# Other numbers in a list scheduler's priority table: a gated recurrence and a low-rank mixer on one core

## The chip, the cores and the metric

The kernel runs on one core of one Trainium2 chip. The metric is the device time of one execution in microseconds (us). Five runs of the kernel before gave 699.36 us in the median, from 696.82 to 702.98. PE is TensorE's matmul stream, PEld its weight loads, DVE is VectorE, ACT is ScalarE, POOL is GpSimd, and SP is the engine that issues most DMAs.

## The reference

```
# attention: q, k, v, a_re, a_im are (4, 8, 768, 48) = batch, heads, seq, dim
mag = sqrt(a_re^2 + a_im^2);  scale = min(mag, 0.999) / (mag + 1e-6)
a = (a_re + i a_im) * scale
for t in range(768):
    S = a[t][:, None] * S + k[t] v[t]^T          # a complex 48x48 state per head
    y[t] = q[t] . Re(S)
# mixer: x = y as (4, 768, 384); U (768, 32), V (32, 768), w_ch1 (384, 1536), w_ch2 (1536, 384)
u = x + ((x^T @ U) @ V)^T
out = u + relu(u @ w_ch1) @ w_ch2
```

All is in 32 bit floats.

## The kernel before

**How the work is cut.** Each of the 4 batches has 768 steps in 6 chunks of 128, so there are 24 chunks, numbered through. Two chunks form a group of gates, so there are 12 groups, and also one unit `m` of the mixer (256 tokens), so there are 12 of those.

For a group, `gates` turns a_re and a_im into the logarithm of the magnitude (tile `GL`) and the angle. Sums of the logarithms are matmuls with fixed triangles (`es ps`, L606, and `tot`, L635), of which ACT takes the exponential (tiles `es` and `E`). Sums of the angles are matmuls too (`ph`, L673 and L676), and ACT takes sine and cosine (tile `cs`). The exponential and the sine need different tables, so ACT loads a table (L345) twice for each group. Four small DMAs of SP (L621) bring `E` into the tile `T`.

For a chunk, `prep` multiplies q and k by `es` and by `cs` on DVE (tiles `qk` and `QKC`), turns them by PE transposes (`tr`, L728), and ACT copies them to `QK` (L731). There is one QKC buffer, so the product for k has to wait for the transposes of q. Then `chain` does the chunk itself:

- a first inner product (`inner`, L762), DVE steps that multiply parts of QK by T (L351), a second inner product, more such steps, a third, more, the corner blocks (`corners`, L812), and one more
- transposes of k (`ks ps`, L834), copied by ACT (L836), and the change of the state (`dk`, L849), which DVE adds up in `GM` and `G`
- the output (`y`, L880 from inside the chunk, L888 from the state), copied by ACT to the tile `xo` (L897)

From group 5 on, the two chunks of a group go through their inner products together.

When all six chunks of a batch are there, the mixer of its three units can begin: `mixed` (L922 and L938) for the low-rank part, a transpose (`uTp`, L951), the first product (`up`, L963, or a form with fewer products, `few`, L1021, in the last six units), the relu on ACT, the second product (`down`, L1109 for the first unit and L1152 for all others), and the sum on DVE.

The two mixer weights come from HBM in 13 pieces, each loaded to `stage` by SP (L501), put through six DVE steps (L510 to L520) and a DMA of POOL (L523).

**What sets the order.** Nothing is emitted as it is written down. Every step is put on a list by `plan.add`, with an engine, a cost, a rank, and what it reads and writes. `Plan.order` then plays the list through: at each moment an engine takes, among the steps that are ready and whose buffers are free, the one with the smallest rank, and prefers, within a margin, one of PE's steps that doesn't change the way the array is split. A step's rank is `urgency(kind, n)`:

```
def urgency(kind, n):
    if kind == "load":
        return n - 20
    if kind in ("totals", "place"):
        return n - 100
    if kind in ("small", "mixing"):
        return n + (1000 if kind == "mixing" else -1000)
    return URGENCY[kind][n]
```

So the products of the mixer come after all else, its small steps before all else, and the rest by the table `URGENCY`, whose kinds are `gates`, `sums` and `angles` (by the first chunk of a group or part), `prep` and `turn`, `levels`, `rest`, `state` and `outs` (by chunk, along the chain), `w1` and `w2` (the steps on the weights), and the loads: `weights` (by piece), `a` (by group), `qk` and `v` (by chunk).

Two things are laid into the order besides. Until the mixer begins, a gap of PE in the plan is filled with a matmul of ones that nothing reads (`spare`, L1276). And the plan holds PE back where a block of 127 of its matmuls would begin before its instruction packet can be there; the five constants for that are `(95, 127, 16, 3.7, 5.0)`.

After that the order of each engine's instructions is fixed.

Of the kernel before, what the change touches and what calls it, by code (L numbers as in the profile page):

```python
# [23 lines left out]
BLK = 32  # L24

URGENCY = {
    "w1": {0: 4.35, 1: 40.16, 2: 150.67, 3: 966.97, 4: 354.88, 5: 201.91, 6: -347.74},
    "w2": {0: 36.04, 2: 316.12, 4: -116.9, 6: 49.42, 8: 239.47, 10: -42.68, 12: 905.56},
    "gates": {0: 106.25, 1: 103.41, 2: -49.5, 4: 87.42, 6: 520.33, 8: -217.02, 10: -47.21, 12: 15.35, 14: 388.43,
        16: 377.04, 18: 75.51, 20: 482.53, 22: -570.43},  # L30
    "angles": {0: -45.95, 1: -31.03, 2: 3.04, 4: 76.17, 6: 325.92, 8: 170.31, 10: -242.52, 12: 333.98, 14: 307.48,
        16: 245.66, 18: -154.27, 20: -22.54, 22: -152.79},
    "prep": {0: 65.38, 1: 12.93, 2: 208.72, 3: -93.77, 4: 100.03, 5: 121.08, 6: 30.53, 7: 497.07, 8: 443.41, 9: 441.88,
        10: 412.66, 11: 327.28, 12: 178.27, 13: 244.54, 14: 74.83, 15: 119.83, 16: 67.35, 17: -210.69, 18: -7.09,
        19: 410.77, 20: -32.17, 21: -59.68, 22: -53.53, 23: 128.41},
    "levels": {0: 41.9, 1: 191.08, 2: 116.73, 3: -50.42, 4: -431.96, 5: -261.25, 6: 94.9, 7: 88.8, 8: -34.01, 9: -85.63,
        10: 13.38, 11: -90.78, 12: -81.71, 13: 119.77, 14: 111.08, 15: 93.04, 16: 48.04, 17: -35.61, 18: -111.26,
        19: 131.26, 20: 11.83, 21: -81.39, 22: -354.36, 23: -91.29},
    "rest": {0: 81.99, 1: -59.7, 2: 1.02, 3: -71.43, 4: 245.98, 5: -217.29, 6: 387.39, 7: 33.15, 8: 464.42, 9: 534.03,
        10: 131.9, 11: -138.5, 12: -136.14, 13: -61.57, 14: -83.99, 15: 843.33, 16: -109.93, 17: 326.93,  # L40
        18: 109.25, 19: -126.18, 20: -0.61, 21: 112.93, 22: -121.98, 23: 76.32},
    "weights": {0: 19.13, 1: -30.23, 2: 81.23, 3: -41.37, 4: 117.09, 5: -154.67, 6: -18.47, 7: -64.05, 8: -71.98, 9: 42.5,
        10: 22.71, 11: -132.3, 12: -28.92},
    "sums": {0: 38.2, 1: 9.35, 2: -20.87, 4: 72.92, 6: -208.53, 8: 13.55, 10: 442.28, 12: 493.43, 14: -34.3,
        16: 584.57, 18: -52.23, 20: -15.92, 22: -382.44},
    "a": {1: 45.05, 2: -60.04, 3: 40.52, 4: -64.28, 5: 71.14, 6: 56.18, 7: 48.88, 8: 43.59, 9: -113.18, 10: -203.48,
        11: 104.55},
    "qk": {0: 21.45, 1: 43.5, 2: -122.7, 3: -37.56, 4: 55.46, 5: 70.35, 6: 197.75, 7: -64.38, 8: 55.95, 9: -154.84,
        10: 75.22, 11: 59.13, 12: 41.58, 13: -8.32, 14: 0.07, 15: -156.61, 16: -54.3, 17: 82.1, 18: -45.58,
        19: -38.55, 20: -58.21, 21: 74.41, 22: 51.81, 23: -3.13},  # L50
    "v": {0: 31.24, 1: -88.34, 2: 92.21, 3: -206.6, 4: -98, 5: 49.22, 6: -34.84, 7: -104.15, 8: 159.93, 9: -122.83,
        10: 61.89, 11: 6.88, 12: 23.97, 13: -44.49, 14: 154.22, 15: 99.08, 16: -48.69, 17: 42.73, 18: -7.23,
        19: 11.85, 20: 11.56, 21: 93.39, 22: 1.68, 23: -27.47},
    "turn": {0: -319.93, 1: 75.52, 2: 97.21, 3: 432.88, 4: 142.09, 5: -31.81, 6: -88.04, 7: -136.12, 8: 41.72,
        9: -25.02, 10: -97.74, 11: -37.55, 12: -241.47, 13: 125.07, 14: -2.5, 15: 87.38, 16: 496.92, 17: -60.29,
        18: 165.32, 19: 552.82, 20: -140.53, 21: 352.69, 22: -223.28, 23: -132.58},
    "state": {0: 945.95, 1: 68.62, 2: 97.42, 3: -70.11, 4: -126.07, 5: -341.17, 6: 128.62, 7: -437.25, 8: 381.46,
        9: 162.75, 10: 823.03, 11: 2.59, 12: -328.28, 13: 333.79, 14: 63.94, 15: 11.18, 16: -228.67, 17: -30.22,
        18: 32.15, 19: -51.58, 20: 49.2, 21: -57.99, 22: -91.91, 23: 89.63},
    "outs": {0: -76.21, 1: 313.36, 2: 356.44, 3: -123.39, 4: 110.21, 5: 113.85, 6: 125.94, 7: -188.23, 8: -30.2,  # L60
        9: -59.92, 10: -1.69, 11: 531.17, 12: -190.52, 13: -532.31, 14: 53.16, 15: -0.59, 16: 32.72, 17: 44.86,
        18: 355.55, 19: 48.52, 20: -58.05, 21: -67.97, 22: 105.42, 23: 31.35},
}


# [1266 lines left out]
```

## Time and profile before

| | us |
|---|---|
| median of 5 runs | 699.36 (696.82 to 702.98) |
| the profiled execution | 701.22 |
| its span, first to last instruction | 699.5 |
| mean granted TensorE clock in it | 0.993 |
| DVE: products on QK (L351), 120 of 1.219 us | 145.5 |
| PE: `up` (L963), 432 records | 98.9 |
| PE: `down` (L1152), the largest form, 396 records | 74.4 |
| PE: `spare` (L1276), 202 records | 53.6 |
| ACT: table loads (L345), 24 of 1.283 us | 30.8 |
| instruction packets (queue q8): 92 packets | 1.51 MB |

A 32-bit matmul of the program shows as two records on PE, a transpose as one. Records are pipelined and their ends are modelled, so a share of busy time on PE isn't a share of its peak. "issue" in a chain of waits is time in which an engine waited for nothing that the profile shows.

### The profile page before, as it was taken

The numbers are of one execution on the slowest core, as the hardware profiler recorded it, in microseconds if no ns is written. First come the engines' busy times: TensorE is split into PE (matmuls) and PEld (weight loads), VectorE is DVE, ScalarE is ACT, GpSimd is POOL, SyncE is SP. The second block draws the span as 40 slices with busy tenths as digits, with TensorE's granted clock in tenths as the row PEclk, the third lists the DMA queues.
The fourth block names the chain that finished last, engine by engine and source line by source line (L and its number), as shares of the span: only waits on it lengthen the run. The fifth ranks groups of instructions, "written<-read, shape, count | busy, mean of one in ns | idle before, by whom it ended". The sixth has DMA issues, their size and how long they took to land.

```text
span 699.5 us, 26207 instructions
## 1 busy us (share of the span) xinstructions
PE 678.6 (97%) x11736; PEld 567.1 (81%) x11736; DVE 541.5 (77%) x886; ACT 415.2 (59%) x776; POOL 47.6 (7%) x84
## 2 busy tenths in 40 slices
PE   9989998999999999999999999999999999999998
PEld 3455666667678888888888888889999999899998
DVE  6899998967997877849769568869887787455734
ACT  7789766667796895857757884642534315131230
POOL 3100000002010010101001010000000000000000
PEclk9999999899999999999999999999999999999999
DMA  7857865657723541431432222131121000000000
GB/s 189 158 162 151 165 131 151 130 136 187 135 63 69 108 100 31 86 65 50 79 74 57 57 53 55 18 76 42 28 43 35 14 29 16 18 7 23 7 18 23
DMA packets 165200, 53.19 MB, mean 76 GB/s; under 512 B 154016, under 2 KB 160352, under 8 KB 165088
## 3 DMA queue, kind: packets, MB, share of 16 engines
q1 hardware_dynamic: 161008, 42.26, 27.6%
q0 software_dynamic: 4080, 9.27, 5.9%
q8 instruction: 92, 1.51, 0.9%
q14 instruction: 20, 0.16, 0.1%
HBM read 33.59 MB, written 4.72 MB: 55 GB/s over the span
## 4 chain that ended last, share of the span: by engine, by line
PE 77%; DVE 11%; ACT 7%; issue 3%; DMA 1%; SPq 1%; DVEq 0%; ACTq 0%
PE down L1152 19%; PE few L1021 12%; PE up L963 11%; PE tr L728 6%; PE inner L762 5%; DVE QK L351 3%; PE y L888 3%; PE dk L849 3%; ACT gate L348 3%; PE spare L1276 2%; PE down L1109 2%; PE ph L673 2%; PE es ps L606 2%; PE ks ps L834 2%; PE y L880 2%
## 5 line engine op out<-in xcount | busy, mean ns | idle before, releaser
L351 DVE TENSOR_TENSOR QK<-QK,T 112x1024 f32<-112x1024 f32 x120 | 145.5, 1219 | 6.8 <-PE corners L812 4.7
L963 PE MATMUL up<-uT,w 128*128 128x256 f32 x432 | 98.9, 381 | 0.2 <-DVE uT L953 0.2
L963 PEld LDWEIGHTS up<-uT,w 128*128 128x128 f32 x432 | 80.3, 190 | 12.1 <-DVE uT L953 0.7
L731 ACT COPY QK<-tr 112x512 f32<-112x512 f32 x96 | 53.2, 587 | 36.2 <-PE tr L728 35.8
L1152 PE MATMUL down<-w,h 128*128 128x192 f32 x396 | 74.4, 331 | 0.0
L348 ACT ACTIVATE gate<-gate 128x768 f32<-128x768 f32 (+1 forms) x91 | 70.3, 791 | 3.6 <-DMA gate<-in_a_re_dram 2.2
L1152 PEld LDWEIGHTS down<-w,h 128*128 128x128 f32 x396 | 63.9, 190 | 2.8 <-issue 1.1
L1029 ACT COPY h<-few 128x512 f32<-128x512 f32 x36 | 20.7, 582 | 74.0 <-PE few L1021 67.3
L762 PEld LDWEIGHTS inner<-QK 112*32 112x32 f32 x4608 | 45.1, 109 | 18.5 <-issue 8.1
L728 PE MATMUL tr<-ident,QKC 128*112 128x128 f32 x384 | 55.0, 280 | 3.3 <-DVE QKC L351 1.9
L354 DVE TENSOR_TENSOR h<-few,h 128x512 f32<-128x512 f32 x54 | 36.9, 690 | 27.3 <-PE few L1021 26.0
L762 PE MATMUL inner<-QK 112*32 112x16 f32 (+1 forms) x4608 | 50.5, 190 | 4.9 <-issue 1.9
L1276 PE MATMUL spare<-ones 128*128 128x512 bf16 x202 | 53.6, 402 | 1.2 <-DVE ones L412 1.2
L728 PEld LDWEIGHTS tr<-ident,QKC 128*112 128x112 f32 x384 | 42.1, 135 | 13.8 <-ACT QK L731 4.7
L351 DVE TENSOR_TENSOR QKC<-qk,cs 128x768 f32<-128x768 f32 x48 | 45.8, 954 | 7.5 <-PE tr L728 7.2
L354 DVE TENSOR_TENSOR xo<-down,xo 128x192 f32<-128x192 f32 (+1 forms) x79 | 29.5, 386 | 21.9 <-PE down L1152 21.6
L897 ACT COPY xo<-y 64x192 f32<-64x192 f32 x96 | 30.0, 312 | 24.6 <-PE y L888 19.3
L1021 PE MATMUL few<-gate,w 128*128 128x128 f32 x336 | 43.0, 277 | 0.0
L768 DVE COPY_PREDICATED DG<-mask,inner 128x128 f32<-128x128 int32 (+1 forms) x72 | 24.1, 342 | 24.1 <-PE inner L762 24.0
L1096 POOL DMA_DIRECT2D out_dram<-xo x32 | 17.9, 560 | 331.6 <-DVE xo L354 315.6
L348 ACT ACTIVATE h<-h 128x512 f32<-128x512 f32 x36 | 22.6, 631 | 30.0 <-DVE h L354 29.9
L1021 PEld LDWEIGHTS few<-gate,w 128*128 128x128 f32 x336 | 39.9, 192 | 0.3
(132 smaller groups left out, 1264.9 us busy)
## 6 DMA issues: line engine op xcount, KB each, us to landing
stage<-in_moe_w_ch_dram SPq DMA_DIRECT2D x12, 768.0 KB, 7.4
gate<-in_a_re_dram SPq DMA_DIRECT2D x24, 192.0 KB, 3.6
gate<-in_a_im_dram SPq DMA_DIRECT2D x24, 192.0 KB, 3.7
qk<-in_q_dram SPq DMA_DIRECT2D x24, 192.0 KB, 3.9
qk<-in_k_dram SPq DMA_DIRECT2D x24, 192.0 KB, 4.2
VP<-in_v_dram SPq DMA_DIRECT2D x24, 192.0 KB, 3.7
T<-E SPq DMA_DIRECT2D x48, 96.0 KB, 2.6
w<-stage POOLq DMA_DIRECT2D x12, 384.0 KB, 5.9
```

The lines of the kernel that those rows point to most:

```text
L348: return nc.scalar.activation(out=o, in_=i, func=f, **kw)
L351: nc.vector.tensor_tensor(out=o, in0=a, in1=b, op=OP.mult)
L354: nc.vector.tensor_tensor(out=o, in0=a, in1=b, op=OP.add)
L728: nc.tensor.transpose(out=get(*ps)[0:DQ, j], in_=get(*qkc)[:, hh * HH + j].rearrange("p u d -> p (u d)")[:, 0:DQ], identity=ident)
L731: ACT(c_act(HH * CH) - 0.05, RT, lambda u=u, hh=hh, ps=ps: nc.scalar.copy(out=get(*QK)[:, u, hh * HH:(hh + 1) * HH], in_=get(*ps)[0:DQ]), ...
L762: nc.tensor.matmul(out=get(*ps)[js, h], lhsT=k_of(h)[:, js], rhs=part(q_of(h)[:, js], "p"), start=True, stop=True, tile_position=(0, j * BLK))
L768: nc.vector.copy_predicated(out=to, mask=part(mask[:, n], "p").unsqueeze(1).to_broadcast(list(to.shape)), data=a if hf < 8 else a.rearrang ...
L897: ACT(c_act(HH * D), RO, lambda r=r, u=u: nc.scalar.copy(out=get(*xi).rearrange("p (a u d) -> p a u d", u=2, d=D)[r * HC:(r + 1) * HC, :, ...
L963: nc.tensor.matmul(out=get(*ps)[:, e], lhsT=w1[:, f, (ff + e) * 128:(ff + e + 1) * 128], rhs=get(*uT)[:, f], start=(f == 0), stop=(f == KD ...
L1021: nc.tensor.matmul(out=get(*ps)[:, q], lhsT=w()[:, q * 128:(q + 1) * 128], rhs=v[0](), start=(n == 0 and q == 0), stop=True, skip_group_ch ...
L1152: nc.tensor.matmul(out=get(*to)[:, part], lhsT=x(j), rhs=y[:, j], start=(first and j == 0), stop=(j == KH - 1), skip_group_check=not first)
L1276: nc.tensor.matmul(out=spare[0], lhsT=ones, rhs=ones.unsqueeze(1).to_broadcast([128, 4, 128]), start=True, stop=True)
```

## The change

Only the table `URGENCY` is changed, and in it every number. No step is added, taken away or costed otherwise; the constants of the plan, the pools and the tiles stay. The kinds and their indices stay too. Some of the lines (the others are changed in the same manner):

```diff
 URGENCY = {
-    "w1": {0: 4.35, 1: 40.16, 2: 150.67, 3: 966.97, 4: 354.88, 5: 201.91, 6: -347.74},
-    "w2": {0: 36.04, 2: 316.12, 4: -116.9, 6: 49.42, 8: 239.47, 10: -42.68, 12: 905.56},
...
+    "w1": {0: -262.78, 1: 77.4, 2: 59.79, 3: 354.47, 4: 165.29, 5: 432.04, 6: 13.21},
+    "w2": {0: -278.56, 2: 142.74, 4: 90.26, 6: -29.83, 8: 309.38, 10: -293.7, 12: 259.97},
...
-    "weights": {0: 19.13, 1: -30.23, 2: 81.23, 3: -41.37, 4: 117.09, 5: -154.67, 6: -18.47, 7: -64.05, 8: -71.98, 9: 42.5,
-        10: 22.71, 11: -132.3, 12: -28.92},
...
+    "weights": {0: 31.74, 1: -38.04, 2: 70.61, 3: -81.71, 4: 89.41, 5: -162.31, 6: -32.16, 7: -31.79, 8: -94.61, 9: 45.12,
+        10: 35.33, 11: -136.44, 12: -8.98},
...
-    "a": {1: 45.05, 2: -60.04, 3: 40.52, 4: -64.28, 5: 71.14, 6: 56.18, 7: 48.88, 8: 43.59, 9: -113.18, 10: -203.48,
-        11: 104.55},
...
+    "a": {1: 49.48, 2: -66.69, 3: 58.41, 4: -63.78, 5: 113.78, 6: 2.5, 7: -13.48, 8: 89.21, 9: -28.67, 10: -233.56,
+        11: 164.57},
```

What this makes of the order is seen when the two built programs are laid side by side, engine by engine. Here is PE ahead of the first `up`, from the `tot` matmuls of the third group on (before, then after; the number counts matmuls, `in` is an inner product, `co` the corners, KS the transposes of k, `yi` and `yb` the lines L880 and L888):

```
before: tot16 TR8 in32 sp2 TR4 sp2 TR4 sp2 in32 ph1 pt1 ph1 in64 pt1 co16 sp7 KS8 in32 dk16 co16 sp6 KS8 sp6 TR8
        yi16 yb8 TR8 yb8 in32 TR4 dk16 in32 TR4 sp11 in32 yi16 yb16 TR8 co16 sp1 in32 sp1 KS8 sp2 in32 dk8 es2
        dk8 tot8 in32 tot8 sp5 co16 sp5 KS8 yi16 yb16 sp1 dk8 ph1 yi16 yb16 sp3 mixed12 sp5 mixed4 sp2 uTp6 sp5 up
after:  tot8 sp1 tot8 in32 TR8 sp6 TR8 in64 ph1 pt1 ph1 co16 in32 pt1 KS8 sp5 dk8 in32 dk8 sp3 co16 sp6 KS4 sp1
        KS4 sp1 TR8 yi16 yb8 TR8 yb8 in32 TR4 dk16 in32 TR4 sp8 yi16 yb8 in32 yb8 TR8 sp3 in32 co16 sp2 es2 in32
        tot8 KS8 tot8 dk16 in32 sp10 co16 yi16 yb16 KS8 sp3 dk8 ph1 yi16 yb16 sp3 mixed12 sp5 mixed4 sp2 uTp6 sp5 up
```

And ACT in the same place, from the last exponentials of the group on:

```
before: es es es es E E table corners(chunk 5) x4 arctan table ks x2 y(chunk 4) x4 ...
after:  E E table arctan table corners(chunk 5) x4 y(chunk 4) x4 ks x2 ...
```

## The prediction

> **What bounds the kernel now.** I read the stages first: three stretches of the span, cut at the first matmul of the mixer (`up`, L963, at 146.86 us) and at the first of L1021 (481.22 us).
>
> ```profile
> PE 678.6 (97%) x11736; PEld 567.1 (81%) x11736; DVE 541.5 (77%) x886; ACT 415.2 (59%) x776; POOL 47.6 (7%) x84
> PEclk9999999899999999999999999999999999999999
> 0.00:146.86 146.86, 133.00 (x2441) 82.50 (x2441) 130.88 (x204) 110.10 (x205) 14.79 (x34) 0.97 0.72 161
> 146.86:481.22 334.36, 330.86 (x6076) 279.50 (x6077) 263.79 (x404) 237.01 (x426) 24.15 (x34) 1.00 0.35 74
> 481.22:699.50 218.28, 214.74 (x3222) 205.10 (x3221) 146.82 (x280) 68.10 (x145) 8.63 (x16) 1.00 0.09 22
> ```
>
> The columns of the last three are the stretch, its length, and the busy time of PE, PEld, DVE, ACT and POOL, then granted clock, DMA share and GB/s. After 146.86 us PE is the bound: it idles 3.50 us of 334.36 and 3.54 of 218.28. Before it, DVE is: 130.88 of 146.86 here, and 69.4 of the 70 us from 35 to 105. PE's 133 us there hold 53.6 us of `spare` matmuls (L1276), which compute nothing. So the time is the moment of the first `up`, plus a body of PE work that no order can shrink, plus little holes.
>
> Next the chain of waits just ahead of the first `up`, and the clock there:
>
> ```profile
> 110.28 0.84 PE y L888 x24
> 111.11 1.68 issue
> 112.80 0.58 PE y L888 x8
> ...
> 125.69 1.28 ACT L345
> ...
> 128.07 0.85 ACT gate L348
> ...
> 128.93 1.28 ACT L345
> ...
> 130.23 0.95 ACT ks L836 x2
> ...
> 131.78 1.77 PE dk L849 x16
> 133.55 1.58 PE ph L673 x2
> 135.13 1.04 PE y L880 x32
> 136.16 1.88 PE y L888 x32
> 138.04 1.39 PE spare L1276 x3
> 139.43 2.48 PE mixed L922 x24
> ```
> ```profile
> 110.00:112.50 2.50, 1.11 (x41) 0.93 (x32) 2.18 (x3) 0.63 (x2) 0.86 (x1) 1.00 0.44 88
> 112.50:115.00 2.50, 2.20 (x16) 1.97 (x16) 1.43 (x2) 1.18 (x3) 0.00 (x0) 0.59 1.01 175
> 130.00:132.50 2.50, 1.98 (x40) 1.62 (x37) 2.50 (x5) 2.42 (x8) 0.00 (x0) 1.00 0.54 128
> 135.00:137.50 2.50, 2.50 (x59) 2.35 (x60) 2.50 (x5) 0.85 (x2) 0.86 (x1) 0.50 1.33 240
> 137.50:140.00 2.50, 2.50 (x19) 0.86 (x19) 1.77 (x3) 1.83 (x5) 0.37 (x1) 0.50 0.84 189
> ```
>
> Two things to see. The clock is halved three windows long, by the trace's clock record from 112.94 to 116.35 and from 133.42 to 140.24 us, each time after some 3.4 us in which PE had almost nothing but the little `y` and `dk` products (64x48). And the last chain runs through ACT (two table loads, 1.28 each, around an arctan of 0.85), then through PE at half clock, where every piece is long.
>
> **The change part by part.** It adds and removes no instruction: PE 6497, DVE 888, ACT 778, POOL 89 and SP 289 program instructions stand in both orders, 202 spares among them. More than that: the work ahead of the first `up` is the same set (202 DVE and 209 ACT instructions before the first `uT` copy and the first relu of `h`; on PE the same number of every kind), and from the first L1021 on PE's order is the same but for one group of eight transposes, which stands behind six `down` and an inner product instead of ahead of them. So nothing moves between the three stages, and the last one (218 us, with its closing 3.5 us of idle) I cost at nothing. What moves is the order inside the first two.
>
> *Start (0 to 35 us).* SP issues q and k of the first chunk ahead of two weight loads of 768 KB, and DVE multiplies q and k by `es` (0.95) where it ran a weight step (0.55). DVE's idle from 12.99 to 14.80, on ACT's GL, stays; by 16.13 (the next thing it waits for) it has done 0.87 of work instead of 0.94. Nothing; without that cover it would be the 0.95.
>
> *The last chain before the mixer.* On ACT both table loads now stand ahead of the four corner copies of chunk 5 instead of one on either side; the four copies of chunk 4's `y` (1.30) stand ahead of the two `ks` copies (0.95) instead of behind them. On DVE two products with `es` and the sum of G stand ahead of chunk 5's last product on QK: from DVE's rows that product ends at 128.24 + 0.87 + 0.47 = 129.6, so KS is 1.3 later, while chunk 4's `y` fills the gap on PE. Counting ACT from the end of E (125.67): 1.28 + 0.85 + 1.28 + 1.06 + 1.30 + 0.95 = 6.72, so `dk` starts at 132.4 instead of 131.78: 0.65 later. But the matmuls of es and tot stand ahead of the ks transposes and of dk, and ACT idled 1.41 + 0.55 + 0.90 = 2.9 us on just these, so E can end that much sooner; then DVE is last, and `dk` starts near 131. Bounds -0.8 and +0.65; I take 0. Behind the ACT copies wait `dk`, then `ph`, `y`, `mixed` and the first `up`, so an error here goes through whole.
>
> *The clock in that chain.* PE's order becomes 10 spares, corners, `y`, eight transposes, 3 spares, `dk`; it was 5 spares, corners, 5 spares, transposes, `y`, 1 spare, `dk`. The window 126.59 to 130.00, with five spares and eight transposes in it, was followed by full clock; the next, with 26 `y` records, one spare and 16 `dk` records, by half. In the new order the transposes and three spares stand inside that stretch. At full clock the pieces from `dk` on cost, by the same kinds elsewhere in the chain of waits: dk 0.92 (122.43), ph 0.65 (half of es x4, 1.29), y 0.61 and 1.07, spares 0.71, mixed 2.09. Against 1.77, 1.58, 1.04, 1.88, 1.39 and 2.48 that is 0.85 + 0.93 + 0.43 + 0.81 + 0.68 + 0.39 = 4.1 us. One weak window can remain (dk, ph and y make 3.25 us in which only ph is dense); it would halve the spares and `mixed` behind it, some 1.4. Bounds: nothing saved, 4.1 saved; a halved window somewhere new costs up to 1.7. I take 4.1 - 1.4 = 2.7.
>
> The Trainium skill ("TensorE: Matmul & The Clock Gate", section "Why this matters for your kernels") asks for no idle gaps of PE over about 3 us between bursts, and would have the clock drop only then. Here the longest gap before a drop is 1.68 us, and before the second drop 0.52: the row speaks against the rule. By the rule no reordering of busy work would touch the clock, and this term would be 0 instead of 2.7.
>
> *Instruction packets.* PE's instructions come in 92 packets of 16 KB. PE stood 1.68 us at 111.11 on "issue", 1.4 us beyond the packet's end at 111.4; in the mixing stage 1.0 once at 419. In the trace a packet lands 0.9 to 6.2 us after the PE record that is 143 records ahead of its first one (19 packets of the first stage, median 3.3; 47 of the second, median 2.2). PE's own work over those 143 records, with the same price for every kind, is shortest at 4.43, 4.66 and 4.98 us in the old order and 4.66, 4.90 and 4.98 in the new one, and at 3.52 against 3.81 in the mixing stage. Averaging the overshoot over those landings, plus 1 us until PE goes on, gives 5.3 before and 4.8 after in the first stage and 0.3 in both in the second. Most of it falls on a PE that waits for DVE anyway. Bounds -1.5 and +1.5; I take 0.4 saved.
>
> The skill ("Runtime: NRT & Kernel Launch", section "Instruction fetch mechanics") holds this fetch to be mostly hidden, sequential and ahead of the issue. The 1.68 us says not here; by the rule this term is 0, which moves the sum by 0.4.
>
> *Mixing stage (146.86 to 481.22).* PE has 501 runs of one kind in the old order, 492 in the new. A run of six `down` records takes 1.17, of twelve 1.95, so a run more costs at most 0.195: 9 of them 0 to 1.75; as ends are modelled I take 0. All of PE's idle there is 3.50, so no more can be gained. Stalls arise where too little PE work lies between dependent steps. Between the two transposes that share the one QKC buffer the thinnest cover was 0.98, 1.55 and 1.60, and is 1.62, 1.62 and 2.08: better. Between the third inner product and the corners of chunk 8 it falls from 3.9 to 1.6, against one DVE product of 1.22 with whatever stands ahead of it; between corners and ks of the pair 10 and 11 from 5.2 to 2.6, against 2.44: worse. Covers of two kinds, two up and two down: 0, with bounds -2 and +2.5.
>
> **Sum.** 2.7 + 0.4 = 3.1 off the profiled execution's own 701.22 us (span 699.5) gives 698.1. That execution is 1.86 over the median of five, 699.36. If its excess is of the same kind as what is saved, the median also ends at 698.1; if not, at 696.3. I take the middle, **697.2**.
>
> **Rivals.**
> *Clearly faster.* The whole 4.1 comes, and the stall at 111.11 and the halved window behind it go too: DVE idled 2.8 us between 110 and 120 on them (0.32 + 1.07 + 0.92 + 0.45 in the slices). 701.2 - 6.9 = 694.3. For it: the new order puts inner products and an earlier return of transposes between the `y` there. Against: PE's work over the 143 records ahead of that packet shrinks from 5.6 to 5.1 us.
> *Slower.* The last chain gets later. Its place is ACT's queue before `dk`: if E does not come sooner, ks copies stand behind KS (1.3 later) and behind all four `y` copies (1.3), and a hole of 2.6 us makes one more halved window (1.7): +4.3 on the median, 703.7. It decides from a first `up` after 150.4 (146.86 + 3.5). For it: the ACT sum of 6.72 above. Against: PE's es and tot are earlier, and `y` covers.
> *It does nothing.* Windows fall as before and the terms cancel: 699.4.
>
> **Chances.** What a measurement of this kernel can tell from no change is about 0.5%, 3.5 us. Forecast 0.35; clearly faster 0.33; slower 0.26 (0.19 by the last chain, 0.07 by the thin covers of the mixing stage, worth at most some 2.5 and a halved window); nothing 0.06. So faster 0.33, same 0.41, slower 0.26. The range for 8 in 10 goes from 691.5 (the faster rival with most of the 3.5 us of idle) to 704.5 (the slower one with 0.8 more); the forecast's own is 695.9 to 699.4.
>
> **What would show it.** Right: in the changed profile the clock column reads 1.00 over most of the 14 us before the first `up`, that `up` starts near 143 to 145 us, the stretch from it to the first L1021 is again 334 us within 2, and the rest 218 us. Wrong: a first `up` at or after 147 us with new halved windows; or a mixing stage longer by over 2 us, with waits on QK or QKC in it; or a gain that sits in the last 218 us, which I hold to be the same.

## The result, and the profile after

The changed kernel takes 703.26 us in the median of 25 runs (700.2 to 705.0), the kernel before 699.44 in the median of 49 runs beside it (696.04 to 703.12). The ratio is 1.0054, with a 95% interval of 1.0040 to 1.0068: 3.8 us slower, more than the 0.5% that can be told from no change. The forecast said 2.2 us faster.

The profiled execution of the changed kernel took 702.21 us (span 700.4), only 1.0 more than the profiled one of before. Its page and its three stages, cut at the first `up` and at the first L1021 as in the prediction, with the same columns:

```profile
PE 676.6 (97%) x11736; PEld 566.9 (81%) x11736; DVE 543.5 (78%) x886; ACT 414.7 (59%) x776; POOL 47.3 (7%) x84
PEclk9999999999999999999999999999999999999999
0.00:145.45 145.45, 129.24 (x2441) 80.99 (x2441) 131.16 (x204) 109.67 (x205) 14.57 (x34) 0.99 0.67 155
145.45:482.05 336.60, 332.33 (x6075) 280.56 (x6076) 265.39 (x405) 236.91 (x426) 24.08 (x34) 0.99 0.36 77
482.05:700.40 218.35, 215.03 (x3223) 205.38 (x3222) 146.99 (x279) 68.12 (x145) 8.63 (x16) 1.00 0.09 21
```

The first `up` comes 1.4 us sooner than before. The prediction cut the old profile at 481.22 us, but the first L1021 begins at 481.06 there; cut at that point as here, the old mixing stage is 334.20 us and the old last stage 218.44. So the last stage is the same, and the mixing stage has grown from 334.20 to 336.60, by 2.40. Next the place that the forecast was about, as the windows show it (granted clock third from the end), and the chain of waits there:

```profile
130.00:132.50 2.50, 2.50 (x73) 2.39 (x74) 2.50 (x4) 2.17 (x8) 0.00 (x0) 1.00 0.36 80
...
135.00:137.50 2.50, 2.50 (x66) 1.90 (x66) 2.50 (x5) 0.82 (x2) 0.45 (x1) 1.00 1.03 201
137.50:140.00 2.50, 2.50 (x31) 0.94 (x29) 2.40 (x5) 1.86 (x5) 0.74 (x1) 1.00 1.03 199
```
```profile
133.27 1.70 PE dk L849 x16
134.97 0.84 PE ph L673 x2
135.82 0.79 PE y L880 x32
136.61 1.07 PE y L888 x32
137.68 0.75 PE spare L1276 x3
138.43 2.07 PE mixed L922 x24
```

Here the forecast holds: the clock reads 1.00, and `ph`, `y`, spares and `mixed` take 0.84, 0.79, 1.07, 0.75 and 2.07 where they took 1.58, 1.04, 1.88, 1.39 and 2.48. Only `dk` isn't shorter (1.70 for 1.77), and it begins 1.5 us later than before (133.27 for 131.78). But two halved windows stand elsewhere, from 60.2 and from 312.8 us by the clock record. The first, in PE's timeline (start, length, operation; in brackets the idle time ahead and what ended it) and in the windows:

```profile
56.41 0.61 PE L888 MATMUL y<-GM,QK 112*64 112x48 f32 x13
60.13 0.42 PE L888 MATMUL y<-GM,QK 112*64 112x48 f32 x3 [3.12 <-issue]
```
```profile
57.00:60.00 3.00, 0.02 (x1) 0.00 (x0) 1.70 (x3) 0.15 (x1) 0.00 (x0) 1.00 0.68 204
60.00:62.50 2.50, 2.37 (x39) 1.37 (x40) 1.91 (x3) 1.83 (x7) 0.00 (x0) 0.54 0.03 7
```

PE stops in the middle of sixteen equal matmuls and waits for nothing that the profile shows. An instruction packet landed at 58.84, and PE goes on 1.29 us later. In all the profiles here, stops of this kind end 1.2 to 1.7 us after the landing of a packet, so I read them as packets that are late. The clock is then halved. The second is in the mixing stage. PE's timeline there, changed kernel first, then the same steps before:

```profile
305.06 2.12 PE L922 MATMUL mixed<-xo,UV 128*32 128x384 f32 x22
307.11 0.91 PE L606 MATMUL es ps<-GL,mid 128*128 128x384 f32 x2
307.86 1.14 PE L1152 MATMUL down<-stage,more 128*128 128x192 f32 x6
308.93 1.27 PE L762 MATMUL inner<-QK 112*32 112x16 f32 x128
312.02 0.95 PE L938 MATMUL mixed<-r,V 64*128 64x192 f32 x8 [1.82 <-issue]
312.90 3.82 PE L1152 MATMUL down<-stage 128*128 128x192 f32 x12
```
```profile
308.87 2.14 PE L922 MATMUL mixed<-xo,UV 128*32 128x384 f32 x24
310.82 1.33 PE L762 MATMUL inner<-QK 112*32 112x32 f32 x128
312.08 0.92 PE L938 MATMUL mixed<-r,V 64*128 64x192 f32 x8
312.94 1.24 PE L1152 MATMUL down<-stage 128*128 128x192 f32 x6
314.01 1.14 PE L1152 MATMUL down<-w,h 128*128 128x192 f32 x6
314.99 0.82 PE L951 MATMUL uTp<-ident,xo 128*128 128x128 f32 x6
315.64 1.14 PE L1152 MATMUL down<-w,h 128*128 128x192 f32 x6
316.71 1.30 PE L762 MATMUL inner<-QK 112*32 112x16 f32 x128
```

The block that begins at record 5549 has its first matmul in L938. In the changed order the 143 records ahead of it take 3.69 us, as they hold an inner product of 128 records that is over in 1.27. The packet landed 4.32 us after the first of them, at 310.64, and PE went on at 312.02. In the old order the same 143 places hold 5.72 us of work, and there is no stop. The work is not the only difference: in the old order that packet landed 2.3 us after the first of its 143 records, 2 us faster than in the changed one, with the DMA engines all but idle in both (shares of 0.03 and 0.01). Why it took longer stays open. After the stop twelve `down` records take 3.82 us, where the two groups of six before take 2.2: the halved window.

### The profile page after: what moved, and what is told of

Same layout as the page of the kernel before. It is cut to its first block, busy times and chain, and to the rows that moved or that the text cites. A ratio compares the mean times of both kernels' runs of the same rounds, so it can differ in the third digit from the quotient of the medians.

```text
span 700.4 us, 26203 instructions
## 1 busy us (share of the span) xinstructions
PE 676.6 (97%) x11736; PEld 566.9 (81%) x11736; DVE 543.5 (78%) x886; ACT 414.7 (59%) x776; POOL 47.3 (7%) x84
## 4 chain that ended last, share of the span: by engine, by line
PE 72%; DVE 15%; ACT 7%; issue 5%; DMA 1%; SPq 0%; DVEq 0%; ACTq 0%
PE down L1152 20%; PE few L1021 12%; PE up L963 10%; PE tr L728 5%; PE inner L762 4%; DVE QK L351 4%; ACT gate L348 3%; PE y L888 3%; PE dk L849 2%; PE down L1109 2%; PE ks ps L834 2%; PE y L880 2%; PE spare L1276 2%; PE ph L673 2%; PE es ps L606 1%
## 5 line engine op out<-in xcount | busy, mean ns | idle before, releaser
L728 PE MATMUL tr<-ident,QKC 128*112 128x128 f32 x384 | 53.3, 277 | 3.1 <-DVE QKC L351 1.5
L1021 PE MATMUL few<-gate,w 128*128 128x128 f32 x336 | 43.1, 277 | 0.0
L1021 PEld LDWEIGHTS few<-gate,w 128*128 128x128 f32 x336 | 39.9, 192 | 0.4
L1276 PEld LDWEIGHTS <-ones 128*128 128x128 bf16 x202 | 19.4, 102 | 23.0 <-issue 6.4
```

Source lines behind the costliest of these rows:

```text
L728: nc.tensor.transpose(out=get(*ps)[0:DQ, j], in_=get(*qkc)[:, hh * HH + j].rearrange("p u d -> p (u d)")[:, 0:DQ], identity=ident)
L1021: nc.tensor.matmul(out=get(*ps)[:, q], lhsT=w()[:, q * 128:(q + 1) * 128], rhs=v[0](), start=(n == 0 and q == 0), stop=True, skip_group_ch ...
L1276: nc.tensor.matmul(out=spare[0], lhsT=ones, rhs=ones.unsqueeze(1).to_broadcast([128, 4, 128]), start=True, stop=True)
```

## The experiments

All medians below are of 6 to 12 runs, beside 23 to 35 runs of the kernel before on the same chip. "Mixing" is the stretch from the first `up` to L1021 in the profile; before it is 334.2, and 334.7 in a second profile. "Stop" is a wait of PE on "issue" at a block's first records that ends 1.2 to 1.8 us after the packet's landing; it is counted from the start of the record ahead of it, and so is some 0.2 us longer than the idle time in brackets (2.00 for the 1.82 above). A block's number can differ by a few records between profiles.

**Which stage loses.** Both kernels again, and both tables in one kernel: the first order up to the first mixer product, where both have done the same steps, then what is left in the second order.

```diff
-    for n in plan.order():
+    for n in two_orders(plan, urgency):
...
+def two_orders(plan, urgency):
+    head = plan.order()
+    plan.urgency = lambda kind, n: REST[kind][n] if kind in REST else urgency(kind, n)
+    late = plan.order()
+    cut = next(x for x, n in enumerate(head) if n >= 0 and plan.ops[n][3][0] == "mixing")
+    done = set(head[:cut])
+    return head[:cut] + [n for n in late if n >= 0 and n not in done]
```

b2 is the kernel before and a2 the changed one; ab has the changed order first, ba has it second.

> The kernel before once more, for a second profile and for the granted clock of each of its executions (each halved window of 3.41 us takes 0.0024 off the mean clock). Both theories: 699.4 in the median, as in the 49 runs. Clock theory: its runs have a mean clock of 0.990 to 0.998, lower on the slow ones, and about as many halved windows as the changed kernel's (2.7 on average), so that the clock explains the spread of each and not the difference. Packet theory: the profile again has PE stopped 3 to 4 us in all on packets that land late (first profile: 1.08, 1.90 and 0.51, and 1.17 at 419 us).

> The changed kernel once more, for a second profile. 703.3 in the median. Packet theory: PE is again stopped some 8 to 10 us in all on late packets (first profile: 3.33, 1.19, 2.15, 1.01 and 2.00), at the same records. Rival (thin covers between dependent steps): the packets' stops differ from profile to profile and the stretch from the first up to the first L1021 is again 2 to 3 us longer than in the kernel before, with waits of PE on DVE or ACT in it.

> The order of the changed kernel up to the first product of the mixer, and from there the order of the kernel before. First-stage theory (packets land late where PE has too little work ahead of them, which then delays DVE): 702 to 703, most of the loss. Rival (the loss is in the mixing stage, and the first stage gains what the clock gives): 697 to 699.4. If both stages lose: about 701.

> The order of the kernel before up to the first product of the mixer, and from there that of the changed kernel. First-stage theory: 699 to 700. Rival (thin covers or late packets in the mixing stage, 336.6 us against 334.2 in the two profiles): 702 to 705. If both stages lose: about 701.

| | median | ratio (95%) | first `up` | mixing | halved windows at | stop at 5549 |
|---|---|---|---|---|---|---|
| b2 | 699.09 | 0.9992 (0.9966 to 1.0018) | 147.16 | 334.66 | 119.5, 133.2 | none |
| a2 | 702.99 | 1.0061 (1.0033 to 1.0088) | 144.03 | 336.78 | 124.4, 312.1 | 2.47 |
| ab | 700.16 | 1.0008 (0.9982 to 1.0035) | 146.01 | 333.49 | 60.4, 115.1 | none |
| ba | 702.45 | 1.0044 (1.0012 to 1.0076) | 146.59 | 335.27 | none | 2.47 |

Whoever has the changed rest loses 2.7 to 2.8 us (ba over the kernel before beside it, 699.74; a2 over ab). So this loss lies behind the first `up`, and the last stage is the same in all (218.1 to 218.6). In the profiles the mixing stage is 3.3 us longer in a2 than in ab, but only 0.6 to 1.1 longer in ba than in the two profiles of before; the stop at record 5549 is there in each. ab, at 700.16, lies between what was expected of a gain and of a loss in the first stage. Not as expected: PE's stops add up to 5.7 us in b2 where 3 to 4 were forecast, and to 7.9 in a2 where 8 to 10 were, with none at record 729.

**More work ahead of the late block.** Two groups of `down` are moved from behind L938 to ahead of the inner product, in the changed order (a_down) and in ba (ba_down).

```diff
-    for n in plan.order():
+    for n in moved(plan.order()):
...
+def moved(out):
+    for n, before in MOVED:
+        out.remove(n)
+        out.insert(out.index(before), n)
+    return out
+
+MOVED = [(718, 1461), (719, 1461)]
```

> The changed kernel, but in the mixing stage two groups of `down` of unit 2 (L1152, twelve records, 2 us of PE work) stand ahead of the second inner product of the pair 12/13 instead of behind the L938 after it. Theory (a late instruction packet): in the changed kernel 143 records of PE took only 3.6 us there, and PE stood 2.0 to 2.5 us ahead of L938 with nothing that it waited for; with 2 us more work inside those records the stop falls to 0.6 us or less, the stretch from the first `up` to L1021 goes from 336.7 to 333.5-334.7, the halved window at 312 us goes too, and the median falls from 703.0 to 699.5-701. Rival (L938 or what is behind it waits for another engine, or the 2.4 us of the mixing stage are spread over many places): the hole only moves or is filled by the same two groups once, L938 starts no earlier than 312 us after the start, and the median stays at 702-703.5.

> The order of the kernel before up to the first mixer product, the changed order from there, and the same two groups of `down` moved as in a_down. Without the move this order took 702.45 with a stop of 2.47 us ahead of L938. Late packet: the stop is gone and the median is 699-700.5, that is the time of the kernel before. Rival: 702-703.

a_down: 702.48 (ratio 1.0048, 1.0023 to 1.0072), mixing 334.93, no halved window after the first `up`. ba_down: 700.70 (1.0030, 1.0001 to 1.0059), mixing 334.91. The stop is gone from a_down and is 0.34 us in ba_down: more work in the 143 records takes it away, as the packet would have it. The medians fell by 0.5 and 1.75 us (0.1 and 1.3 when each is taken over the kernel before beside it), not by 2 to 3, and neither fall is clear of noise: a_down went as its rival said, and ba_down lies between. PE's timeline of a_down at the same place shows one reason:

```profile
312.72 1.27 PE L762 MATMUL inner<-QK 112*32 112x16 f32 x128
313.92 0.92 PE L938 MATMUL mixed<-r,V 64*128 64x192 f32 x8
315.99 1.01 PE L951 MATMUL uTp<-ident,xo 128*128 128x128 f32 x6 [1.15 <-DVE xo L354]
```

The work that filled the stop is missing between L938 and the transposes, which need DVE's sum of L938's result. The stop had covered part of a wait for DVE.

**The place within the blocks alone.** In the kernel before, the last fill matmuls ahead of the mixer are cut into halves (18 of them, b_split) or quarters (20, b_split60). No step changes its place; the blocks shift by 18 and 60 records.

```diff
+        for r in ((0, 2), (2, 4)) if 740 <= x < 828 else ((0, 4),): nc.tensor.matmul(out=spare[0][:, r[0]:r[1]], ...)
```

> The kernel before with each of the last 18 fill matmuls (`spare`) ahead of the first mixer product cut into two halves of 256 columns: the same columns, the same order, every step in its place, but 18 records more, so that each block of 127 records in the mixing stage begins 18 records earlier in the order. Theory (packets): what a block's place costs depends on the work in the 143 records before it; replaying the 48 blocks of the mixing stage at places 18 records earlier, with the times from request to go that this stage showed, gives 7.3 us of stops in place of 2.7, so the stretch from the first `up` to L1021 grows by 3 to 6 us and the median goes to 702.5-706. Rival (order and dependencies alone set the time of the mixing stage): within 0.5 us of the kernel before.

> As b_split, but the last 20 fill matmuls are cut into four quarters of 128 columns, so that the mixing stage stands 60 records later in the blocks instead of 18. By the replay of the 48 blocks the stops of the mixing stage are then 13 us instead of 2.7 in the kernel before (for 18 records it gave 7.3, and the median rose by 5.5). Theory (place within the blocks): the median is 706 to 713. Rival (finer fill work or a lower clock made b_split slow, not the place): no more than b_split's 704.8.

b_split: 704.79 (1.0069, 1.0042 to 1.0096); b_split60: 710.74 (1.0159, 1.0121 to 1.0196). Both medians lie in the ranges given: 5.5 and 12.0 us for the same work in the same order. The clock is a small part of that: its mean is 0.9927 and 0.9947 where the runs beside them have 0.9960 and 0.9962, which is 1.8 and 0.8 us at the price worked out below. Mixing is 337.45 and 346.14, and there are stops where there were none, as in `tot` of b_split:

```profile
190.33 0.68 PE L635 MATMUL tot<-total,GL 128*64 128x64 f32 x15
193.21 0.27 PE L635 MATMUL tot<-total,GL 128*64 128x64 f32 x1 [2.21 <-issue]
```

In the kernel before the sixteen records of this `tot` run through in 0.69 us. b_split60 has eight stops of 0.5 to 2.4 us in mixing. So where the 127-record blocks begin is a term of its own, worth 12 us at the worse of these two places.

**A more careful plan.** The changed table with 5.0 in place of 3.7 in the plan's constants for packets.

```diff
-    plan = Plan(0.04, 0.12, 4.0, (3.0, 0.23, 0.4), 2.0, urgency, (95, 127, 16, 3.7, 5.0))
+    plan = Plan(0.04, 0.12, 4.0, (3.0, 0.23, 0.4), 2.0, urgency, (95, 127, 16, 5.0, 5.0))
```

> The changed table with a plan that counts 5.0 instead of 3.7 us from a block's request to its first record in the mixing stage too. The order changes from the middle of the mixing stage on. Theory (packets cost the changed table its loss there): stops in the mixing stage fall, and the median is 0.5 to 2.5 us below the changed kernel's, unless the more cautious order opens holes of its own. Rival (dependencies): no better than 702.5.

A miss: 717.57 (1.0270, 1.0230 to 1.0311), mixing 351.55, with stops of 1.0 to 2.7 us at five places in it. The new order is another order, not the same one with wider covers.

**Filling what comes out behind it.** a_fix moves five groups of `down`: a_down's two, one between L938 and the transposes, and one each ahead of the stops at 3647 and 4027. ba_fix does this in ba. a_fix6 moves one more, ahead of `tot`. b_fix moves three in the kernel before, ahead of its own holes.

```diff
+MOVED = [(718, 1461), (719, 1461), (721, 1227), (655, 1004), (667, 1014)]  # a_fix, ba_fix
+MOVED = [(718, 1461), (719, 1461), (721, 1227), (655, 1004), (667, 1014), (722, 1551)]  # a_fix6
+MOVED = [(655, 913), (702, 1180), (1319, 1745)]  # b_fix
```

> The changed kernel with five of its steps moved in the mixing stage, all of them groups of `down` (L1152): two ahead of the second inner product of the pair 12/13, as in a_down; one of unit 2 between L938 and the transposes `uTp`, since in a_down PE stood 1.47 us there for the sum on DVE; one of unit 1 ahead of the corners of chunk 8; one of unit 1 ahead of the `dk` of chunk 8. The last two put 1 us more PE work into the 143 records ahead of the stops at records 3647 and 4027 (1.0 and 0.4 to 1.2 us in the changed kernel's profiles). Theory (late packets make the loss in the mixing stage): the stretch from the first `up` to L1021 is 332.5 to 334.3 us, at or under the kernel before's 334.2 to 334.7, with no halved window in it, and the median is 699.5 to 701.3, the time of the order with only the first stage changed (700.16). Rival (other waits of the changed order hold it back): the stretch stays at 334.9 or more and the median at 702 or more.

> The same five moves on the order that has the first stage of before and the changed rest. Theory: 698 to 700, the kernel before's time or up to 1.5 us under it, since the stops of the mixing stage are then smaller than those of before. Rival: 700.7 as ba_down, or more.

> The kernel before with three groups of `down` moved: one ahead of the last transposes of chunk 17, which puts 1 us more work into the 143 records ahead of record 7329 (stop of 1.17 to 1.55 us) and fills a wait of 0.73 us of these transposes; one ahead of the `dk` of chunk 7 (stop of 0.5 us at record 3647); one ahead of the corners of the pair 10/11 (wait of 0.5 us). Theory (stops and holes of PE in the mixing stage pass to the end one for one): the stretch from the first `up` to L1021 goes from 334.4 to 331.8-333.3, and the median is 1 to 2.5 us under the kernel before's. Rival (what is moved only shifts a wait to its former place): within 0.5 us of the kernel before.

> a_fix with one more group of `down` of unit 2 moved, ahead of the `tot` matmuls that in a_fix waited 1.48 us for the copy of `uTp` on DVE. Theory (with the packet's stop gone, what is left of the loss at this place is that wait): the wait falls to 0.3 to 0.7 us, the stretch from the first `up` to L1021 from 335.2 to 334.0-334.7, the median to 700.5-702. Rival: DVE is as late for the next step as for this one, the stretch stays within 0.3 us of 335.2.

| | median | ratio (95%) | mixing | stops in mixing |
|---|---|---|---|---|
| a_fix | 702.34 | 1.0035 (1.0012 to 1.0058) | 335.22 | 0.33 |
| ba_fix | 700.93 | 1.0017 (0.9992 to 1.0042) | 334.94 | none |
| a_fix6 | 702.57 | 1.0041 (1.0011 to 1.0070) | 335.00 | none |
| b_fix | 700.30 | 1.0015 (0.9989 to 1.0040) | 334.57 | 1.41 |

None of the four theories holds. The rivals hold in a_fix, ba_fix and a_fix6; b_fix ends 1.5 us over the kernel before, where its rival allowed 0.5, and its interval doesn't tell that from nothing. In the changed order the packets' stops are all but gone from the mixing stage, but mixing is stuck at 335. The wait moves on. In PE's timeline of a_fix, then of a_fix6:

```profile
312.89 1.01 PE L951 MATMUL uTp<-ident,xo 128*128 128x128 f32 x6
315.22 1.15 PE L635 MATMUL tot<-total,GL 128*64 128x64 f32 x32 [1.31 <-DVE uT L953]
```
```profile
316.47 1.15 PE L635 MATMUL tot<-total,GL 128*64 128x64 f32 x32 [0.34 <-DVE uT L953]
317.56 1.24 PE L1152 MATMUL down<-w,stage 128*128 128x192 f32 x6
319.53 1.43 PE L762 MATMUL inner<-QK 112*32 112x16 f32 x128 [0.73 <-DVE QK L351]
```

First the sum, then the copy, then the product on QK: DVE is late for each in turn. What a_fix's median still loses isn't seen there, as its profiled execution took 699.19, some 3.2 less than that median. b_fix is another case. Its stop at record 7329 stayed (1.41 us, after 1.17 and 1.55 in the kernel before), since the `down` moved there filled a wait of 0.73 us that already lay within the same 143 records: without the stop they take 5.89 us now and took 5.73. The packet lands 5.9 us after the first of them, with loads of q and k in flight.

**Cuts further back.** The tables change at the first mixer product of unit 3, where the old order has done all that the new has but eleven steps. b3a goes from old to new, a3b from new to old; ab3a is b3a with the changed first stage.

```diff
+PARTS = [(3, TABLE_0)]  # b3a, a3b
+PARTS = [(0, TABLE_0), (3, TABLE_1)]  # ab3a
...
+    for unit, table in PARTS:
+        cut = next(x for x, n in enumerate(out) if n >= 0 and plan.ops[n][3] == ("mixing", unit))
```

> The order of the kernel before up to the first mixer product of unit 3, the changed order for all that is left. At that point the changed order has done the same steps and eleven more of the pair 12/13 and of the gates. Theory (the loss sits at one place, the inner products of the pair 12/13 with L938 of unit 3 between them, which come ahead of this cut; behind it the changed order is no worse: 157.9 against 160.5 us with 1.3 us of PE work less left to do): the stretch from the first `up` to L1021 is 332.5 to 334.7 us and the median 697.5 to 700. Rival (the changed order loses by small waits all along, in the later units too): 701 or more.

> The reverse: the changed order up to the first mixer product of unit 3, the order of before for the rest. Theory: the stop of 2.0 to 2.5 us at record 5549 is there, the stretch is 336.5 to 338.5 us, and the median 702 to 704.5. Rival: 699.5 to 701.

> The changed order up to the first mixer product, that of before for units 0 to 2, the changed order for the rest: b3a with the other first stage. As the order with only the first stage changed took 0.4 to 1.1 us more than before (interval from 1.2 less to 2.4 more), the theory that the changed first stage gains nothing gives 0 to 1.5 us more than b3a. My forecast's clock term, if it holds, gives 2.7 us less than b3a.

a3b: 704.62 (1.0061, 1.0035 to 1.0087), mixing 337.07 with a stop of 2.20 at 5549, as expected. b3a: 701.67 (1.0025, 0.9995 to 1.0055), mixing 336.49; ab3a: 703.59 (1.0046, 1.0020 to 1.0072), mixing 336.64. a3b shows that the changed order has lost ahead of unit 3's first mixer product. ab3a takes 1.9 us more than b3a, where a first stage that gains nothing was to give 0 to 1.5 more and my clock term 2.7 less. b3a misses: it has no packet's stop in mixing, but at the seam the third inner product of the pair 12/13 is brought too close behind the second:

```profile
317.02 0.73 PE L762 MATMUL inner<-QK 112*32 112x16 f32 x64 [0.34 <-DVE QK L351]
319.42 1.05 PE L762 MATMUL inner<-QK 112*32 112x16 f32 x64 [1.67 <-DVE QK L351]
320.40 3.81 PE L963 MATMUL up<-uT,w 128*128 128x256 f32 x11
```

and the eleven `up` records behind it take 3.81 us at half clock. So b3a doesn't tell whether the later units of the changed order lose too. It does show again that too little PE work between the inner products of this pair leaves PE waiting for DVE.

**The first stage.** ab_load is ab with the weight piece issued at 52 us put behind the last `v` load; ab2 is ab again.

```diff
+    out.remove(37)
+    out.insert(out.index(391) + 1, 37)
```

> The order with the changed first stage and the rest of before (ab, 700.16), with one load moved: SP issues the weight piece of 768 KB not at 52 us but behind the last `v` load, at about 57 us. In the changed order the loads of a, q, k, v and this piece are issued from 49.2 us on, and in seven of nine profiles of the changed first stage the instruction packet for record 729 landed at 57.3 to 59.6 us instead of 51.2 to 52.6 (two of nine with the first stage of before, whose loads are issued 1.5 us later), so that PE stood 2.0 to 3.3 us at 57 us, in most of them with a halved window behind it. Theory (the packet lies behind these loads): without the piece among them it lands by 56 us at the latest, the stop at record 729 is under 0.5 us, there is no halved window at 58 to 62 us, and the median is 1 to 2 us under that of the order beside it, 698 to 699.5, at or under the kernel before. Rival (the packet's second landing time has nothing to do with this load): stop and median as in ab.

> ab again, beside ab_load: 699.7 to 701.5, and by the odds so far a stop of 2 to 3 us at record 729 in its profile.

ab_load: 700.20 (1.0006, 0.9980 to 1.0032), ab2: 700.64 (1.0021, 0.9999 to 1.0043). The packet for record 729 landed at 57.99 in ab_load too, and PE stopped 2.06 us; so this piece is not what it waits for. The profile of ab_load has no halved window at all, but the median isn't lower by more than can be told. ab2 went as expected, with a stop of 2.5 us there.

No version beat the kernel before.

## Why the prediction was wrong

The range held the time, but the direction was wrong. The slower rival's 703.7 is close, and for another reason: it needed a first `up` after 150.4, and that came at 145.45 and 144.03.

**Last stage: 0.** Right: 218.44 and 218.35.

**Start and last chain: 0.** Right in the main: the first `up` lies near or in the 143 to 145 us that were named, with no hole ahead of `dk`. But in the changed kernel's own profile `dk` begins 1.5 us later than before, past the bound of +0.65; in a2 it is 0.1. That goes with the packet for record 729, whose landing time varies: in the nine profiles in which it landed early, `dk` begins at 131.0 to 132.4 us with either first stage, and in the eleven others at 132.0 to 136.7.

**Mixing stage: 0, bounds -2 and +2.5.** This is the step that failed. The profiles of the two kernels show +2.4 and +2.1, inside the bound but not 0; the medians of pairs with the same first stage (ba over before, a2 over ab) show +2.7 and +2.8, just past it. I looked for thin covers between dependent steps at chunk 8 and the pair 10/11. The largest stop sits at the pair 12/13, where the changed order has two inner products of 128 records with only L922, es and six `down` between them. Without that stop mixing is still 0.2 to 1 us longer than before, as waits for DVE take its place. That work ahead of a block decides over a stop is shown (a_down, b_split); how much of the 2.8 us is the packet and how much the waits behind it is not, since taking the stops away moved no median clear of noise.

**Packets: 0.4 saved, "0.3 in both" in the mixing stage.** The mechanism was known and its size wrong. I averaged the overshoot over all landings, as if each block drew one (median 2.2 us). But a block comes at the same place in each execution, and the one with 3.69 us of work ahead of it, near the shortest that I had counted for the new order (3.81), met a packet that took 4.3 to 5.0 us: record 5549 stopped PE in all four profiles that have this order there (the changed kernel, a2, ba and a3b), for 2.0 to 2.5 us. The stops in mixing add up to 3.4 us in each of the changed kernel's two profiles and to 1.7 and 2.1 in those of before (records 3647 and 7329), and in both profiles of the changed kernel, though not in ba and a3b, a halved window of 1.3 us comes on top. In the first stage they are 4.4 us in the mean of nine profiles that begin with the old order and 5.6 in ten that begin with the new: 1.2 more where I had 0.5 less.

**Clock: 2.7 saved.** Right at the place, wrong in the sum. From the first `dk` to the first `up` it is 12.1 to 12.4 us in all eleven profiles that begin with the changed order. In those that begin with the old one it is 15.1 to 15.2 in five of nine, and 12.1 in the other four, which have no halved window there: the 2.9 us are only saved where the old order would have had it. The 0.85 for `dk` in the 4.1 was misread, as `dk` began at 131.78 and ran at full clock up to 133.42. I priced the windows of one profiled execution and held a new one elsewhere for a bound only. Every run has a mean clock, and a halved window of 3.41 us takes 0.0024 off it (half of 3.41 in 700). In 150 runs of the kernel before the time goes as 697.05 us plus 0.555 for each 0.001 of clock, so a window costs 1.3, with whatever stop goes with it. Full clock (0.999 or more) was seen in 48 of these 150 runs, in 19 of 72 runs of the six kernels here that begin with the old order and leave the fill work whole (0 of 17 with it cut), in none of 127 runs that begin with the changed order, and in 2 of 12 of ab_load. The mean clock is 0.9957 before and 0.9933 after (37 runs): 1.3 us lost. One of the new windows begins at 58 to 63 us, in 8 of 10 profiles of the changed first stage and 1 of 9 of the old; one at 312, behind the stop at 5549. Within a profile, halved windows begin a whole number of 3.41 us apart (74 of them from 60.20 to 312.78), and where this grid lies differs from one execution to the next. That could be why the same stop is followed by a window in one profile and not in another, but no run tests it.

**Is the first stage slower?** Five pairs with the same rest (ab and before, a2 and ba, a_down and ba_down, a_fix and ba_fix, ab3a and b3a) differ by 0.4, 0.5, 1.8, 1.4 and 1.9 us, the changed first stage always the slower one, though each alone is within its noise. With ab2 (1.8) the mean is 1.3. With 2.8 for the rest that makes 4.1, against 3.8 measured. Yet in the profiles the first `up` comes 1.1 us sooner on average (145.25 against 146.35, over the same ten and nine). The clock explains about half of that: the profiles of both groups have a mean clock of 0.994, but the runs of the same kernels have 0.9931 with the changed first stage and 0.9951 with the old, so that the profiles lie 0.5 us under and 0.7 us over their runs by the clock alone. The rest stays open.

**The sum.** It was taken between "the profiled run's excess comes off too" and "it doesn't". The profiled run of before was 1.8 above the median of the 49 runs, that of the changed kernel 1.05 below its own: one profile of each hides 2.8 of the 3.8 us.

The Trainium skill ("TensorE: Matmul & The Clock Gate", section "Why this matters for your kernels") warns of idle gaps over about 3 us. The gap ahead of the window at 60 us was 3.1, and agrees; ahead of the one at 312 it was 1.8, and so a shorter one can come before a drop too, though ba and a3b had a gap of 2.3 and 2.0 at that place without one.

## What to carry to other kernels

Where PE runs many short matmuls, lay the instruction blocks over its order and look at each block: the work in the records ahead of it has to outlast its packet. A block with too little work ahead of it stopped PE in each of its four profiles (record 5549), while one whose packet lands late only at times did not (record 729). Averages over blocks hide this, and adding or removing a few records anywhere shifts all blocks behind it. When a stop is filled with work from its neighbourhood, see first what that work was covering, and take the clock from many runs instead of one profile.

## What was not expected of the hardware

- Cutting 18 or 20 fill matmuls, with order and columns unchanged, cost 5.5 and 12.0 us.
- PE goes on 1.2 to 1.6 us after the packet has landed at both places shown (records 729 and 5549), in every profile that stops there.
- The packet for record 729 has two landing times, 51.4 to 52.8 us or 57.5 to 59.6, with nothing between in 20 profiles: late in nine of the eleven with the changed first stage and in two of the nine with the old. The late one comes when the loads are nearly through (DMA share 0.68 from 57 to 60 us in the changed kernel, 0.03 from 60 to 62.5); what decides was not found.
